# Rearranging the last sixty microseconds of a streaming decode kernel: transfer order, deferred work, a direct last P.V, and closer weight columns

## The chip, the cores and the metric

The kernel runs on one core of a Trainium2 chip. The metric is the device time of one execution in microseconds (us). The profile's span, which runs from the first to the last recorded event, is about 1.8 us shorter than the time of the same execution.

## The reference, cut to what matters

One token goes through a transformer layer. The parts that matter are the sizes.

```
x: 1 x 512                      32 query heads, 8 key/value heads, head size 128
k_cache, v_cache: 8 x 65536 x 128, bf16   (134 MB each)
mod = silu(c) @ w_mod           -> six vectors of 512
h   = layernorm(x) * (1+ca) + sa
q   = h @ wq                    (512 x 4096)
o   = softmax(q k^T / sqrt(128)) v        for each of the 32 heads
x   = x + ga * (o @ wo)         (4096 x 512)
h2  = layernorm(x) * (1+cb) + sb
x   = x + gb * ((silu(h2 @ w_gate) * (h2 @ w_up)) @ w_down)     (512 x 1792, 1792 x 512)
```

Every weight and every cached key and value is read once: 285.48 MB. The output is one row of 512 numbers.

## The kernel before

The caches are cut into 32 chunks of 16384 keys, four to each key/value head. One chunk of K is 4 MB and so is one of V. All large transfers are issued from one queue (SyncE) in a fixed order, a list called `stream`. A store in SBUF of 24 units holds six chunks; `pump` issues the next transfer of the list as soon as enough neighbouring units have been given back by `done`.

```python
UNIT = 4096
UNITS = 24
V_END = (0, 64, 96, 112, 128)               # the last V comes in four pieces
PV_RUNS = ((10, 0, 16), (14, 16, 32))
# ...
    for i in range(NCH + 2):                # NCH = 32 chunks
        if i >= 2:
            kv("v", A_v_cache, i - 2, V_END if i - 2 == NCH - 1 else (0, NB))
        if i < NCH:
            kv("k", A_k_cache, i)
        if NCH + 1 - len(wo_at) <= i <= NCH:
            g0 = wo_at[i - (NCH + 1 - len(wo_at))]
            w(("o", g0), wo3, g0, g0 + WO_G)
    w(("g",), B_w_gate.rearrange("(p k) n -> p k n", p=P), 0, KC)
    w(("u",), B_w_up.rearrange("(p k) n -> p k n", p=P), 0, KC)
    w(("d",), B_w_down.rearrange("(p k) n -> p k n", p=P), 0, FC, (0, FC0, FC))
```

So the end of the stream is ..., V29, K31, (output weights), V30, (output weights), V31, w_gate, w_up, w_down.

For every chunk TensorE transposes K, computes scores, and multiplies the softmax weights P with V. That last product ("P.V") is done as 32 wide matmuls. Each takes four blocks of keys at once and so leaves a 128 x 512 result, of which only matching blocks are wanted. VectorE copies it, and four small matmuls in fp32 (`pv_fold`; the trace counts them as eight) pick out and add the wanted parts.

```python
    def pv_one(cc, q4):
        nc.tensor.matmul(out=pvw[32 * jt:32 * jt + QB * rep, :],
                         lhsT=pt_of[cc][:, b0:b0 + QB, :].rearrange("p b h -> p (b h)"),   # 16 columns
                         rhs=held[("v", cc)][:, b0:b0 + QB, :].rearrange("p j d -> p (j d)"),  # 512
                         # ...
        if q4 == NQ - 1:
            done(("v", cc))
            nc.vector.tensor_copy(out=pvw_sb[:], in_=pvw[:])
```

After the last chunk this has to be followed, one thing after the other, by the copy, the fold, the weights of the four chunks (`head_out`), a turn of the result (`head_turn`), the output projection of the last head, the layernorm, w_gate and w_up, the activation, w_down, and the output transfer.

The feed-forward weights are used as the stationary side of 128 x 128 matmuls with one moving column (`gemv`). Of each row of w_gate and w_up, one matmul takes the columns `strided(held[key][:, kc, :], FC)[:, :, nb]`. With FC = 14 these are every 14th column.

## Time and profile before

| | before |
|---|---|
| median of the first six runs | 693.92 us (692.95 to 696.38) |
| span of the profiled run | 693.8 us |
| bytes streamed | 285.48 MB |
| last V piece landed | 665.2 us |
| last w_down piece landed | 678.1 us |
| h2 (the input of w_gate and w_up) ready | 680.8 us |

These are the lines of the page of the kernel before on which this rests. The row "DMA" is the busy share of the 16 DMA engines in tenths, in 40 slices of the span; the queue lines give packets, MB, and the share of the 16 engines' time.

```profile
span 693.8 us, 18060 instructions
...
DMA  9999999999999999999999999999999999999960
...
q1 hardware_dynamic: 11648, 285.48, 96.2%
q8 instruction: 63, 1.03, 0.6%
```

The stream fills all slices but the last two: the kernel is bound by its input for 660 us and by something else for the rest. The queue q8 carries instructions, not data.

The next view of the kernel before cuts the end into stretches. Its columns are the stretch, its length, the busy time of PE (with its number of instructions), PEld, DVE, ACT and POOL, the granted TensorE clock, the DMA share, and GB/s.

```profile
400.00:500.00 100.00, 89.83 (x1207) 78.12 (x1204) 41.42 (x89) 31.17 (x82) 0.00 (x0) 0.74 1.00 429
660.00:665.00 5.00, 2.30 (x31) 1.86 (x28) 2.61 (x10) 0.93 (x5) 0.00 (x0) 0.74 0.99 406
665.00:670.00 5.00, 4.28 (x118) 4.26 (x122) 0.71 (x4) 2.17 (x7) 0.00 (x0) 0.50 0.63 264
670.00:675.00 5.00, 4.20 (x40) 1.59 (x38) 0.69 (x1) 0.00 (x0) 0.00 (x0) 0.59 0.51 210
675.00:680.00 5.00, 1.94 (x23) 1.67 (x24) 1.98 (x11) 0.21 (x1) 0.48 (x1) 0.64 0.15 58
680.00:685.00 5.00, 4.15 (x70) 4.15 (x70) 0.62 (x3) 0.00 (x0) 0.08 (x1) 0.50 0.00 0
```

In the body the DMA engines are at 1.00 and move 429 GB/s. From 665 us on the share is near one half, although there is still data to move: some of the 16 engines have finished and others have not. Each of the 78 transfers of queue q1 is split over 16 engines (the trace has 1248 closing packets of 4 bytes, 16 for each), and the trace has the time at which each engine finished its share. For the last piece of w_down these 16 times are, sorted:

```
665.0 665.1 665.1 665.2 665.6 665.9 669.4 671.9 675.8 675.9 677.3 677.4 677.4 677.5 677.6 678.1
```

Six engines end at 665 us and eight at about 677. What waits for a transfer here waits for the slowest engine. So the end of the stream (called E) is 678.1 us and not 665.

The last view of the kernel before is its timeline of the tail. The columns are start, busy time (both in us), engine, line, operation, what is written from what, the shape, the number of instructions, and in brackets how long the engine had been idle and what ended that.

```profile
652.78 1.58 PE L371 MATMUL pvw<-store,pt 128*16 128x512 bf16 x16 [3.72 <-DMA store<-in_A_v_cache_dram]
...
666.17 3.86 PE L472 MATMUL attn_ps<-oF,store 128*128 128x1 bf16 x112
669.96 3.59 PE L371 MATMUL pvw<-store,pt 128*16 128x512 bf16 x32
673.61 0.69 DVE L379 COPY pvw_sb<-pvw 128x512 f32<-128x512 f32 x1 [6.35 <-PE pvw L371]
674.35 1.15 PE L389 MATMUL oc<-sel,pvw_sb 128*128 128x4 f32 x8 [0.80 <-DVE pvw_sb L379]
...
676.94 0.67 PE L472 MATMUL attn_ps<-oF,store 128*128 128x1 bf16 x16 [0.25 <-DVE oF L429]
...
680.64 0.16 DVE L518 TENSOR_TENSOR h2T<-m,modT 128x4 bf16<-128x4 f32 x1
680.85 6.83 PE L205 MATMUL gu_ps<-h2T,store 128*128 128x1 bf16 x112 [1.73 <-DVE h2T L518]
688.77 2.03 PE L539 MATMUL f_ps<-guT,store 128*128 128x1 bf16 x56
691.58 0.36 SPq L548 DMA_DIRECT2D out_dram<-o_bf  x1
```

TensorE last waits long for data at 652.78 us, when V30 lands. After that it works through scores, projection and P.V in the order of the program. From the last scores (661.6) to 665.7 us it mostly waits: in three waits of 0.78, 0.62 and 2.01 us for VectorE and ScalarE, which make the softmax of the last chunk. The projection of seven heads doesn't need that softmax, but it stands behind it in the program. When the last V piece is there (665.2), TensorE isn't free for it until 669.96. Note also the two rates: 112 matmuls of the output projection (columns 4 apart) take 3.86 us, which is 34 ns each, and 112 of w_gate and w_up (columns 14 apart) take 6.83 us, 61 ns each.

### The profile page before, as it was taken

What the parts mean: (1) busy time and instruction counts of PE and PEld (TensorE: products, weight loads), DVE (VectorE), ACT (ScalarE), POOL (GpSimd) and SP (SyncE); (2) the same over time, 40 slices, a digit from 0 to 9 for tenths busy, and PEclk for the clock granted to TensorE, in tenths of its full rate; (3) what the DMA queues carried; (4) which work ended last, traced back from release to release, by engine and by line L of the source; (5) the groups of instructions that cost most, each with busy time, mean ns of one, the idle gap of its engine ahead of it and who ended that gap; (6) DMA issues with size and microseconds to landing.
All of it is one profiled execution on the core that took longest, in us unless ns stands there. A gap on an engine that the chain in (4) does not pass through costs nothing.

```text
span 693.8 us, 18060 instructions
## 1 busy us (share of the span) xinstructions
PE 582.6 (84%) x8084; PEld 505.6 (73%) x8084; DVE 264.0 (38%) x604; ACT 200.1 (29%) x527; POOL 3.6 (1%) x17
## 2 busy tenths in 40 slices
PE   1599897988989898988889799888988998887776
PEld 1588786777878787877777688777876787776655
DVE  2154344433434335343444345333443433432331
ACT  0043133332322333333223233332323332321310
POOL 1000000000000000000000000000000000000000
PEclk9988778775867768687768868776877776877765
DMA  9999999999999999999999999999999999999960
GB/s 387 423 423 436 431 427 428 429 429 432 426 430 431 428 435 422 427 433 433 426 424 437 427 427 427 430 431 428 431 425 434 429 428 425 421 435 425 413 289 5
DMA packets 11729, 286.63 MB, mean 413 GB/s; under 512 B 1282, under 2 KB 1284, under 8 KB 2692
## 3 DMA queue, kind: packets, MB, share of 16 engines
q1 hardware_dynamic: 11648, 285.48, 96.2%
q8 instruction: 63, 1.03, 0.6%
q14 instruction: 14, 0.11, 0.0%
q10 hardware_dynamic: 4, 0.00, 0.0%
HBM read 285.48 MB, written 0.00 MB: 411 GB/s over the span
## 4 chain that ended last, share of the span: by engine, by line
issue 97%; PE 2%; DMA 1%; DVE 0%; POOLq 0%; POOL 0%; ACTq 0%; ACT 0%
PE gu_ps L205 1%; DMA store<-in_A_x_dram 1%; PE f_ps L539 0%; PE ln_tot L215 0%; POOLq L574 0%; PE ln_var L224 0%; POOL ln_rstd L228 0%; ACTq L158 0%; DVE xn L513 0%; PE xc_ps L188 0%; PE o_ps L545 0%; PE o_ps L533 0%; DVE xd L218 0%; ACT sg L526 0%; DVE gu_bf L524 0%
## 5 line engine op out<-in xcount | busy, mean ns | idle before, releaser
L308 PE MATMUL ktp<-ident_f,store 128*128 128x128 f32 x2048 | 393.1, 325 | 54.5 <-DMA store<-in_A_k_cache_dram 54.4
L308 PEld LDWEIGHTS ktp<-ident_f,store 128*128 128x128 f32 x2048 | 255.1, 160 | 88.4 <-issue 83.1
L314 DVE COPY kts<-ktp 128x512 int32<-128x512 int32 x256 | 177.1, 692 | 305.4 <-PE ktp L308 304.5
L312 ACT COPY kts<-ktp 128x512 f32<-128x512 f32 x256 | 151.2, 591 | 450.9 <-PE ktp L308 448.6
L329 PEld LDWEIGHTS <-kts 128*128 128x128 bf16 x4096 | 196.1, 102 | 16.6 <-ACT kts L312 1.4
L329 PE MATMUL st<-qpair,kts 128*128 128x8 bf16 x4096 | 185.1, 169 | 1.2 <-ACT kts L312 1.2
L371 PE MATMUL pvw<-store,pt 128*16 128x512 bf16 x1024 | 76.4, 427 | 13.9 <-DMA store<-in_A_v_cache_dram 13.8
L361 ACT ACTIVATE pt<-st,negb 128x128 bf16<-128x128 f32 x128 | 51.2, 556 | 5.5 <-DVE negb L354 5.4
L371 PEld LDWEIGHTS <-pt 128*16 128x16 bf16 x1024 | 22.4, 94 | 33.0 <-issue 17.0
L379 DVE COPY pvw_sb<-pvw 128x512 f32<-128x512 f32 x32 | 22.1, 692 | 44.7 <-PE pvw L371 44.7
L389 PE MATMUL oc<-sel,pvw_sb 128*128 128x4 f32 x256 | 36.4, 265 | 1.0 <-DVE pvw_sb L379 0.8
L389 PEld LDWEIGHTS oc<-sel,pvw_sb 128*128 128x128 f32 x256 | 33.6, 206 | 4.5 <-DVE pvw_sb L379 1.7
L361 ACT ACTIVATION_READ_ACCUMULATOR pt<-st,negb 128x1 f32 x128 | 36.3, 283 | 0.0
L205 PEld LDWEIGHTS <-store 128*128 128x128 bf16 x336 | 13.9, 127 | 13.7 <-DMA store<-in_A_wq_dram 8.5
L336 DVE TENSOR_REDUCE mx<-st 128x4 f32<-128x512 f32 x32 | 21.8, 681 | 0.2 <-PE st L329 0.2
L341 PE MATMUL mt<-ident_f,mx 128*4 128x128 f32 x32 | 10.5, 329 | 9.8 <-DVE mx L336 8.2
L351 PE MATMUL mb<-dg,ones_f 4*128 4x4 f32 x64 | 14.1, 289 | 0.6 <-DVE dg L345 0.6
L343 DVE TENSOR_REDUCE m<-mt 4x1 f32<-4x128 f32 x32 | 8.9, 279 | 13.5 <-PE mt L341 13.5
L351 PEld LDWEIGHTS mb<-dg,ones_f 4*128 4x128 f32 x64 | 11.3, 220 | 1.7 <-DVE dg L345 0.8
L391 DVE COPY oT<-oc 128x4 f32<-128x4 f32 x32 | 5.2, 162 | 18.1 <-PE oc L389 18.1
L341 PEld LDWEIGHTS mt<-ident_f,mx 128*4 128x4 f32 x32 | 2.6, 82 | 12.6 <-DVE mx L336 12.6
L205 PE MATMUL q_ps<-m_h,store 128*128 128x1 bf16 x128 | 3.6, 165 | 8.5 <-DMA store<-in_A_wq_dram 8.5
(98 smaller groups left out, 87.2 us busy)
## 6 DMA issues: line engine op xcount, KB each, us to landing
store<-in_A_k_cache_dram SPq DMA_DIRECT2D x32, 4096.0 KB, 43.4
store<-in_A_v_cache_dram SPq DMA_DIRECT2D x31, 4096.0 KB, 52.3
store<-in_A_wq_dram SPq DMA_DIRECT2D x1, 4096.0 KB, 19.5
store<-in_A_wo_dram SPq DMA_DIRECT2D x4, 1024.0 KB, 46.0
store<-in_w_mod_dram SPq DMA_DIRECT2D x1, 3072.0 KB, 10.2
store<-in_A_v_cache_dram SPq DMA_DIRECT2D x1, 2048.0 KB, 45.6
store<-in_B_w_gate_dram SPq DMA_DIRECT2D x1, 1792.0 KB, 29.6
store<-in_B_w_up_dram SPq DMA_DIRECT2D x1, 1792.0 KB, 31.4
```

The costliest lines, as they stand in the source:

```text
L205: nc.tensor.matmul(out=out_ps[:, nb:nb + 1], lhsT=lhs(kc, nb), rhs=actT[:, kc:kc + 1], start=(kc == 0), stop=(kc == n_kc - 1))
L308: nc.tensor.transpose(out=ktp[:, e4, :], in_=kt32[:, j0:j0 + 2, :].rearrange("p a i -> p (a i)"), identity=ident_f[:])
L312: nc.scalar.copy(out=kts[:].bitcast(F32), in_=ktp[:])
L314: nc.vector.tensor_copy(out=kts[:].bitcast(I32), in_=ktp[:].bitcast(I32))
L329: nc.tensor.matmul(out=st[:, b0:b0 + 2, :].rearrange("p b h -> p (b h)"), lhsT=ktsv[:, e4, :, e], rhs=qpair[:, g, e, :, :].rearrange("p j ...
L336: nc.vector.tensor_reduce(out=mx[:], in_=st_of[cc][:].rearrange("p b h -> p h b"), axis=AX.X, op=ALU.max)
L341: nc.tensor.transpose(out=mt[:], in_=mx[:], identity=ident_f[:])
L351: nc.tensor.matmul(out=mb[:], lhsT=ones_f[0:rep, :], rhs=dg[:], start=True, stop=True)
L361: nc.scalar.activation(out=pt_of[cc][:, :, h], in_=st_of[cc][:, :, h], func=ACT.Exp, bias=negb[:, h:h + 1], scale=scale, accum_out=Lp[:, c ...
L371: nc.tensor.matmul(out=pvw[32 * jt:32 * jt + QB * rep, :], lhsT=pt_of[cc][:, b0:b0 + QB, :].rearrange("p b h -> p (b h)"), rhs=held[("v", ...
L379: nc.vector.tensor_copy(out=pvw_sb[:], in_=pvw[:])
L389: nc.tensor.matmul(out=oc_ps[:], lhsT=pvw_sb[:, bl * Dh:(bl + 1) * Dh], rhs=sel[:, bl, :], start=(bl == 0), stop=(bl == QB - 1))
```

## The change

The intent is to have less work left when the last data arrives. There are four parts.

1. The store's units are halved (48 of 2048), so that smaller transfers fit more tightly. It still holds six chunks.
2. The end of the transfer order changes. The last K goes ahead of V29. P.V of chunks 29 and 30 is deferred: it runs after the last scores instead of among them.
3. The last chunk's P.V is done directly: 128 matmuls with a block of V as the stationary side and 4 columns of P moving. The result has the form that the output projection needs, so the copy, the fold and the turn are gone. The last head's output weights come in a layout to match, in 1 KB packets.
4. The matmuls of w_gate and w_up take columns 4 apart instead of 14 (2 apart in the last 256 columns). w_down's rows are arranged to match, and come in three pieces.

```diff
-UNIT = 4096
-UNITS = 24
+UNIT = 2048
+UNITS = 48
-V_END = (0, 64, 96, 112, 128)
+V_END = (0, 64, 112, 128)
 # ... transfer order
+    order[order.index(("v", NCH - 3)):] = [("k", NCH - 1), ("v", NCH - 3), ("ol",),
+                                           *(o for o in order[order.index(("k", NCH - 1)):] if o[0] == "o"),
+                                           ("v", NCH - 2), ("v", NCH - 1)]
 # ... columns of w_gate and w_up, 4 apart
+    fblocks = [(f0, min(4, (F - f0) // P)) for f0 in range(0, F, 4 * P)]
+    def fcols(w2):
+        return [w2[:, f0:f0 + e * P].rearrange("p (m e) -> p m e", e=e)[:, :, i] for f0, e in fblocks for i in range(e)]
 # ... when P.V runs
+        if cc == NCH - 1:
+            continue
+        if cc == NCH - 3:
+            runs = [END, END + 1]
+        if cc == NCH - 2:
+            runs = [END + 7, END + 8]
 # ... the projection of seven heads between them
+    at(END + 3, attn_begin)
 # ... the last chunk
+    for b in range(NB):
+        nc.tensor.matmul(out=ol_ps[:], lhsT=v_l[:, b, :], rhs=pt_l[:, b, :], start=(b == 0), stop=(b == NB - 1))
+    nc.vector.tensor_tensor(out=ol[:], in0=ol_ps[:], in1=wgt[:, NCPH - 1, :], op=ALU.mult)
+    nc.vector.tensor_tensor(out=ol_bf[:], in0=ol[:], in1=rest[:], op=ALU.add)
+    for nb in range(KC):
+        for h in range(rep):
+            nc.tensor.matmul(out=attn_ps[:, nb:nb + 1], lhsT=strided(wl[:, h, :], KC)[:, :, nb],
+                             rhs=ol_bf[:, h:h + 1], start=False, stop=(h == rep - 1), skip_group_check=True)
 # ... rest of the change cut: the loading of w_down and of the last head's output weights
```

`END` is the step of the last scores.

More of the change, by code (lines that the diff above doesn't have):

```diff
@@ L90, in room @@
         fits = [u for u in range(0, UNITS - n + 1, n) if all(free[u:u + n])]
-        return min(fits, key=lambda u: (sum(free[u // 4 * 4:u // 4 * 4 + 4]), u)) if fits else None
+        return min(fits, key=lambda u: (sum(free[u // 8 * 8:u // 8 * 8 + 8]), u)) if fits else None
     def pump():
@@ L133, in load @@
             return v
-        stream.append((key, max((k1 - k0) * n, 4 * UNIT if key == ("mod",) else 0), load))
+        stream.append((key, max((k1 - k0) * n, 8 * UNIT if key == ("mod",) else 0), load))
     w(("mod",), w_mod.rearrange("(p k) n -> p k n", p=P), 0, KC)
     w(("q",), A_wq.rearrange("(p k) n -> p k n", p=P), 0, KC)
+    GROWS = rep * Dh
     wo3 = A_wo.rearrange("(g p j) n -> p g (j n)", p=P, j=rep)
-    wo_at = list(range(0, Hkv, WO_G))
-    for i in range(NCH + 2):
+    wo_last = A_wo[(Hkv - 1) * GROWS:, :].rearrange("(h d) n -> d h n", d=P)
@@ L141 @@
+    wo_at = {max(0, NCH - 4 + i): (g0, min(g0 + WO_G, Hkv - 1)) for i, g0 in enumerate(range(0, Hkv - 1, WO_G))}
+    order = []
+    for i in range(NCH):
         if i >= 2:
-            kv("v", A_v_cache, i - 2, V_END if i - 2 == NCH - 1 else (0, NB))
-        if i < NCH:
-            kv("k", A_k_cache, i)
-        if NCH + 1 - len(wo_at) <= i <= NCH:
-            g0 = wo_at[i - (NCH + 1 - len(wo_at))]
-            w(("o", g0), wo3, g0, g0 + WO_G)
+            order.append(("v", i - 2))
+        order.append(("k", i))
+        if i in wo_at:
+            order.append(("o", *wo_at[i]))
@@ new lines @@
+    order[order.index(("v", NCH - 3)):] = [("k", NCH - 1), ("v", NCH - 3), ("ol",),
+                                           *(o for o in order[order.index(("k", NCH - 1)):] if o[0] == "o"),
+                                           ("v", NCH - 2), ("v", NCH - 1)]
+    for o in order:
+        if o[0] == "k":
+            kv("k", A_k_cache, o[1])
+        elif o[0] == "v":
+            kv("v", A_v_cache, o[1], V_END if o[1] == NCH - 1 else (0, NB))
+        elif o[0] == "o":
+            w(("o", o[1]), wo3, o[1], o[2])
+        else:
+            w(("ol",), wo_last, 0, rep)
@@ L148, with d_load @@
     w(("g",), B_w_gate.rearrange("(p k) n -> p k n", p=P), 0, KC)
     w(("u",), B_w_up.rearrange("(p k) n -> p k n", p=P), 0, KC)
-    FC0 = FC - 4
-    w(("d",), B_w_down.rearrange("(p k) n -> p k n", p=P), 0, FC, (0, FC0, FC))
-    at0 = 3 * UNIT
+    fblocks = [(f0, min(4, (F - f0) // P)) for f0 in range(0, F, 4 * P)]
+    def fcols(w2):
+        return [w2[:, f0:f0 + e * P].rearrange("p (m e) -> p m e", e=e)[:, :, i] for f0, e in fblocks for i in range(e)]
+    def d_load(t):
+        v = t[:, 0:FC * D].rearrange("p (j n) -> p j n", n=D)
+        full = [f0 for f0, e in fblocks if e == 4]
+        nf = len(full)
+        for b0, b1 in ((0, nf - 1), (nf - 1, nf)):
+            nc.sync.dma_start(out=v[:, 4 * b0:4 * b1, :].rearrange("p (b e) n -> p b (e n)", e=4),
+                              in_=B_w_down[b0 * 4 * P:b1 * 4 * P, :].rearrange("(b p e) n -> p b (e n)", p=P, e=4))
+        if FC > 4 * nf:
+            nc.sync.dma_start(out=v[:, 4 * nf:FC, :].rearrange("p e n -> p (e n)"),
+                              in_=B_w_down[nf * 4 * P:F, :].rearrange("(p e) n -> p (e n)", p=P))
+        return v
@@ L154 @@
+    FC0 = FC // 4 * 4
+    stream.append((("d",), FC * D, d_load))
+    at0 = 6 * UNIT
     c_row = store[0:1, at0:at0 + D]
@@ L442 @@
     NBANKS = NCH * BPC
-    TAIL_AT = NBANKS + S_LAG + 6
-    def late(step):
-        return step if step < NBANKS else step + TAIL_AT - NBANKS
+    END = NBANKS + S_LAG - 1
     for cc in range(NCH):
@@ L454 @@
             at(e + 3 + h // 2, lambda cc=cc, h=h: sm_exp(cc, carry[("nb", cc)], h))
-        for i, a, b in PV_RUNS:
-            at(late((cc + 1) * BPC + i), lambda cc=cc, a=a, b=b: pv_run(cc, a, b))
-        p1 = late((cc + 1) * BPC + PV_RUNS[-1][0] + 1)
+        g = cc // NCPH
+        if cc % NCPH == NCPH - 1:
+            at(e + 6, keep(("wgt", g), lambda g=g: head_weights(g)))
+        if cc == NCH - 1:
+            continue
+        runs = [(cc + 1) * BPC + i for i, _, _ in PV_RUNS]
+        if cc == NCH - 3:
+            runs = [END, END + 1]
+        if cc == NCH - 2:
+            runs = [END + 7, END + 8]
+        for step, (_, a, b) in zip(runs, PV_RUNS):
+            at(step, lambda cc=cc, a=a, b=b: pv_run(cc, a, b))
+        p1 = runs[-1] + 1
         at(p1, lambda cc=cc: pv_fold(cc))
         if cc % NCPH == NCPH - 1:
-            g = cc // NCPH
-            at(e + 6, keep(("wgt", g), lambda g=g: head_weights(g)))
             at(p1 + 1, keep(("om", g), lambda wgt, g=g: head_out(g, wgt), ("wgt", g)))
@@ L473, in wo_part @@
                                      rhs=oF[:, g, j:j + 1], start=(g == 0 and j == 0 and nb == 0),
-                                     stop=(g == Hkv - 1 and j == rep - 1), skip_group_check=True)
+                                     stop=False, skip_group_check=True)
     def attn_begin():
@@ L479, in attn_begin @@
         wo_part(0, Hkv - 1)
-    side.setdefault(TAIL_AT, []).insert(0, attn_begin)
+    at(END + 3, attn_begin)
     last = max(side)
@@ L489 @@
             fn()
-    wo_part(Hkv - 1, Hkv)
-    for g0 in range(0, Hkv, WO_G):
+    gl = Hkv - 1
+    wgt = carry.pop(("wgt", gl))
+    oT = heads.pop(gl)[2]
+    rest = once.tile([P, rep], F32, name="rest", tag="rest")
+    if NCPH > 1:
+        ow = once.tile([P, NCPH - 1, rep], F32, name="ow_l", tag="ow_l")
+        nc.vector.tensor_tensor(out=ow[:], in0=oT[:, 0:NCPH - 1, :], in1=wgt[:, 0:NCPH - 1, :], op=ALU.mult)
+        nc.vector.tensor_reduce(out=rest[:], in_=ow[:].rearrange("p c h -> p h c"), axis=AX.X, op=ALU.add)
+    else:
+        nc.vector.memset(rest[:], 0.0)
+    v_l, pt_l = held[("v", NCH - 1)], pt_of.pop(NCH - 1)
+    ol_ps = pmisc.tile([P, rep], F32, name="ol_ps", tag="misc")
+    for b in range(NB):
+        nc.tensor.matmul(out=ol_ps[:], lhsT=v_l[:, b, :], rhs=pt_l[:, b, :], start=(b == 0), stop=(b == NB - 1))
+    done(("v", NCH - 1))
+    ol = once.tile([P, rep], F32, name="ol", tag="ol")
+    nc.vector.tensor_tensor(out=ol[:], in0=ol_ps[:], in1=wgt[:, NCPH - 1, :], op=ALU.mult)
+    ol_bf = once.tile([P, rep], BF16, name="ol_bf", tag="ol_bf")
+    nc.vector.tensor_tensor(out=ol_bf[:], in0=ol[:], in1=rest[:], op=ALU.add)
+    wl = held[("ol",)]
+    for nb in range(KC):
+        for h in range(rep):
+            nc.tensor.matmul(out=attn_ps[:, nb:nb + 1], lhsT=strided(wl[:, h, :], KC)[:, :, nb],
+                             rhs=ol_bf[:, h:h + 1], start=False, stop=(h == rep - 1), skip_group_check=True)
+    for g0 in range(0, Hkv - 1, WO_G):
         done(("o", g0))
+    done(("ol",))
     warm = once.tile([P, 1], F32, name="warm", tag="warm")
@@ L520 @@
     for i, key in enumerate((("g",), ("u",))):
-        gemv(gu_ps[:, i, :], lambda kc, nb: strided(held[key][:, kc, :], FC)[:, :, nb], h2T, KC, FC)
+        cols = [fcols(held[key][:, kc, :]) for kc in range(KC)]
+        gemv(gu_ps[:, i, :], lambda kc, nb: cols[kc][nb], h2T, KC, FC)
         done(key)
@@ L535 @@
     wd_sb = held[("d",)]
-    for f0, f1 in ((0, FC0), (FC0, FC)):
+    for f0, f1 in ((0, FC0 - 4), (FC0 - 4, FC0), (FC0, FC)):
         for nb in range(KC):
```

## The prediction

> **What bounds the kernel.** The inbound DMA stream. The queue table shows 285.48 MB on one queue, 96% of 16 engines' span; the stretches from 40 to 640 us all read 429 GB/s at a DMA share of 1.00. [...]
>
> The engines do not end together. Each transfer's 16 completion events show eight engines about 12 us behind the fastest at the end. The last weights (w_down) land between 665.0 and 678.1 us; from 665 on the DMA share is near 0.5. The instruction queue (63 packets of 16 KB, 1.07 us each) may explain most of the lag. The laggards set the end of the stream, E = 678.1 us.
>
> From E to the end of the span (693.8 us) is 15.7 us, and that is exposed compute. The timeline of the tail: attention output weights 666.2-670.0, last P.V 670.0-673.6 (its last V piece had landed at 665.2), copy, fold, head output and last output projection to 677.6, layernorm to 680.8, gate and up 6.8 us, activation and setup 1.1, down 2.0, final combination 0.75, output DMA 2.2.
>
> **What the change does.** Bytes and engines' work are the same, so E should stay, plus about 0.3 us: 1 KB packets take 45 ns and 4 KB ones 161 ns, against 1215 for 32 KB (packet records), and the last output weights and w_down now come in smaller packets. The finer units keep six 4 MB blocks; the body does not change.
>
> The last K is moved ahead of two V blocks, landing about 5 us earlier (near 633), and two P.V passes move behind the last scores. Then projection of seven heads and P.V of chunk 30 run while V31 is landing (660-665). V31 goes straight through 128 four-column matmuls piece by piece; I estimate 35 ns each, from the output projection's 112 in 3.9 us. The fold, head turn and transposition vanish: after the last V piece about 0.6 (last 16 blocks) + 0.6 + 0.7 (output projection) + 3.2 (layernorm) us, so h2 is ready near 671, possibly 672, not 680.8. Gate lands near 669.4, up near 673.7. Gate and up drop from 61 ns a matmul (columns 14 elements apart) to about 35 (4 apart, as the down matmuls: 56 in 2.0 us): 6.8 becomes 4 us. Up ends near 675.8, activation near 676.9, down 2.0 us more, almost together with E.
>
> **Sum.** Compute after E shrinks from 15.7 to about 3.5-4 us: end near 681.9 us of span, 12 us less. E is a floor. Predicted 682.0 us (-1.7%), just short of 2%.
>
> **Signs.** E at 677-679; landing of w_down last, and the down matmuls waiting for it; gate/up near 35 ns; P.V of chunk 31 waiting for V pieces, not for TensorE; body at 429 GB/s; no idle DMA before 664.
>
> **What would make it wrong.** Direct P.V at 60 ns at the half clock (stretches after 664 read PEclk 0.5) would delay h2 to about 674 and add 2 us. Deferred P.V passes might hold V blocks so long that w_down is issued late. Fewer instruction fetches on the laggards near the end could bring E forward by 1-2 us and carry it past 2%.
>
> Chances: faster by over 2% 0.18, within 2% 0.81, slower 0.01. Range 679.6 to 685.0.

## The result, and the profile after

The kernel after took 683.37 us (median of 8 runs, 682.97 to 683.71) against 694.24 us of the kernel before (16 runs, 692.95 to 696.38). The ratio is 0.9844, with a 95% interval of 0.9833 to 0.9855: the change is 1.6% faster, which is within 2%. Ratios in this document are the mean time of one kernel's runs over that of the other's runs of the same rounds, so they are not quite the ratio of the medians that are quoted.

The page of the kernel after, the same lines:

```profile
span 681.6 us, 18237 instructions
...
DMA  8999999999999999999999999999999999999994
...
q1 hardware_dynamic: 12176, 285.48, 98.0%
q8 instruction: 64, 1.05, 0.6%
```

The bytes are the same, the idle slices at the end are nearly gone, and there is one more packet of instructions. The same stretches of the kernel after:

```profile
400.00:500.00 100.00, 90.41 (x1203) 79.33 (x1202) 41.16 (x90) 31.46 (x82) 0.00 (x0) 0.80 1.00 428
660.00:665.00 5.00, 4.09 (x125) 4.00 (x126) 0.77 (x4) 0.00 (x0) 0.00 (x0) 0.78 0.99 407
665.00:670.00 5.00, 1.89 (x42) 1.77 (x39) 1.96 (x11) 0.21 (x1) 0.55 (x1) 0.50 0.61 254
670.00:675.00 5.00, 3.36 (x102) 3.27 (x101) 0.00 (x0) 0.00 (x0) 0.00 (x0) 0.50 0.51 206
675.00:680.00 5.00, 2.90 (x74) 2.62 (x71) 0.78 (x5) 0.21 (x1) 0.00 (x0) 0.50 0.19 73
```

The DMA columns of the first four rows agree with those before to 4%: the stream was not made faster, in its body or in its end. What changed is what TensorE does beside it. The clock of this profiled run was 0.823 on average and that of the profiled run before 0.763. But the runs of the kernel before that had clocks of 0.81 to 0.84 took 693.01 to 695.58 us, all over 9 us more than any run of the kernel after, so the clock is not what the change did.

The timeline of the tail of the kernel after:

```profile
647.70 1.90 PE L400 MATMUL pvw<-store,pt 128*16 128x512 bf16 x32
...
651.70 3.89 PE L506 MATMUL attn_ps<-oF,store 128*128 128x1 bf16 x112
655.97 3.55 PE L400 MATMUL pvw<-store,pt 128*16 128x512 bf16 x32
...
661.24 1.76 PE L538 MATMUL ol_ps<-pt,store 128*128 128x4 bf16 x64
663.59 1.87 PE L538 MATMUL ol_ps<-pt,store 128*128 128x4 bf16 x64 [0.59 <-DMA store<-in_A_v_cache_dram]
665.91 0.68 PE L547 MATMUL attn_ps<-ol_bf,store 128*128 128x1 bf16 x16 [0.45 <-DVE ol_bf L543]
669.61 0.17 DVE L576 TENSOR_TENSOR h2T<-m,modT 128x4 bf16<-128x4 f32 x1
669.83 1.95 PE L234 MATMUL gu_ps<-h2T,store 128*128 128x1 bf16 x56 [1.74 <-DVE h2T L576]
673.42 1.98 PE L234 MATMUL gu_ps<-h2T,store 128*128 128x1 bf16 x56 [1.64 <-DMA store<-in_B_w_up_dram]
...
676.49 2.03 PE L598 MATMUL f_ps<-guT,store 128*128 128x1 bf16 x56
679.30 0.36 SPq L607 DMA_DIRECT2D out_dram<-o_bf  x1
```

The projection of seven heads, which ran from 666 to 670 us, now runs from 652 to 656, before the last V is there. It and P.V of chunk 29 fill the time in which the last chunk's softmax is made (until about 654 us). P.V of the last chunk waits for V and not V for TensorE. And between the two halves of line 234 there is a wait for w_up's landing: TensorE has caught up with the stream. Side by side, read from the two traces:

| us from the start of the span | before | after |
|---|---|---|
| scores of the last chunk done | 661.6 | 647.8 |
| last V piece landed | 665.2 | 664.8 |
| P.V of the last chunk done | 673.6 | 665.5 |
| last output projection done | 677.6 | 666.6 |
| h2 ready | 680.8 | 669.8 |
| w_up landed | 673.7 | 673.4 |
| w_gate and w_up used | 687.7 | 675.4 |
| last w_down piece landed (E) | 678.1 | 677.8 |
| w_down used | 690.8 | 678.5 |
| end of the span | 693.8 | 681.6 |

### The profile page after: what moved, and what is told of

It reads as the page before. It is cut to its first block, busy times and chain, and to the rows that moved or that the text cites. A ratio compares the mean times of both kernels' runs of the same rounds, so it can differ in the third digit from the quotient of the medians.

```text
span 681.6 us, 18237 instructions
## 1 busy us (share of the span) xinstructions
PE 578.7 (85%) x8171; PEld 508.7 (75%) x8171; DVE 262.3 (38%) x602; ACT 201.8 (30%) x527; POOL 3.6 (1%) x17
## 3 DMA queue, kind: packets, MB, share of 16 engines
q1 hardware_dynamic: 12176, 285.48, 98.0%
q8 instruction: 64, 1.05, 0.6%
## 4 chain that ended last, share of the span: by engine, by line
DMA 66%; PE 29%; DVE 2%; issue 1%; ACT 1%; another core or an unknown queue 0%; SPq 0%; DVEq 0%; ACTq 0%
DMA store<-in_A_k_cache_dram 55%; PE ktp L337 18%; DMA store<-in_A_v_cache_dram 7%; PE st L358 5%; DMA store<-in_B_w_up_dram 5%; PE pvw L400 4%; DVE kts L343 1%; DVE mx L365 1%; PE mb L380 1%; PE mt L370 1%; PE oc L418 0%; PE gu_ps L234 0%; PE f_ps L598 0%; ACT pt L390 0%
## 5 line engine op out<-in xcount | busy, mean ns | idle before, releaser
L337 PE MATMUL ktp<-ident_f,store 128*128 128x128 f32 x2048 | 398.0, 327 | 57.6 <-DMA store<-in_A_k_cache_dram 57.6
L337 PEld LDWEIGHTS ktp<-ident_f,store 128*128 128x128 f32 x2048 | 266.2, 165 | 85.2 <-issue 78.3
L400 PE MATMUL pvw<-store,pt 128*16 128x512 bf16 x992 | 67.2, 395 | 4.5 <-DMA store<-in_A_v_cache_dram 4.4
L400 PEld LDWEIGHTS <-pt 128*16 128x16 bf16 x992 | 20.5, 90 | 22.1 <-issue 7.3
L418 PE MATMUL oc<-sel,pvw_sb 128*128 128x4 f32 x248 | 32.7, 255 | 2.4 <-DVE pvw_sb L408 1.4
L418 PEld LDWEIGHTS oc<-sel,pvw_sb 128*128 128x128 f32 x248 | 30.0, 191 | 6.1 <-DVE pvw_sb L408 2.5
L234 PEld LDWEIGHTS <-store 128*128 128x128 bf16 x336 | 10.7, 112 | 15.4 <-DMA store<-in_A_wq_dram 8.6
L380 PE MATMUL mb<-dg,ones_f 4*128 4x4 f32 x64 | 15.6, 312 | 0.1
L380 PEld LDWEIGHTS mb<-dg,ones_f 4*128 4x128 f32 x64 | 12.8, 249 | 1.4
```

Of the source, the lines that this page charges most:

```text
L234: nc.tensor.matmul(out=out_ps[:, nb:nb + 1], lhsT=lhs(kc, nb), rhs=actT[:, kc:kc + 1], start=(kc == 0), stop=(kc == n_kc - 1))
L337: nc.tensor.transpose(out=ktp[:, e4, :], in_=kt32[:, j0:j0 + 2, :].rearrange("p a i -> p (a i)"), identity=ident_f[:])
L380: nc.tensor.matmul(out=mb[:], lhsT=ones_f[0:rep, :], rhs=dg[:], start=True, stop=True)
L400: nc.tensor.matmul(out=pvw[32 * jt:32 * jt + QB * rep, :], lhsT=pt_of[cc][:, b0:b0 + QB, :].rearrange("p b h -> p (b h)"), rhs=held[("v", ...
L418: nc.tensor.matmul(out=oc_ps[:], lhsT=pvw_sb[:, bl * Dh:(bl + 1) * Dh], rhs=sel[:, bl, :], start=(bl == 0), stop=(bl == QB - 1))
```

## The experiments

The theory to be tested is that of the prediction. The stream's end stays where it is, and the whole gain is compute that no longer comes after it, in three shares: the order with the deferral, the direct P.V, the columns. The first rival is that one share does it all, or that the shares do not depend on each other. The second question is why the stream's end stays at 678 us when six of its engines are done at 665. The theory there is the instruction fetch; the rival is that these engines are slow for the data itself.

### One share taken away

The kernel after with the columns 14 apart again:

```diff
-        cols = [fcols(held[key][:, kc, :]) for kc in range(KC)]
-        gemv(gu_ps[:, i, :], lambda kc, nb: cols[kc][nb], h2T, KC, FC)
+        gemv(gu_ps[:, i, :], lambda kc, nb: strided(held[key][:, kc, :], FC)[:, :, nb], h2T, KC, FC)
```

> The changed kernel with the columns of gate and up read 14 elements apart again (w_down's rows to match, still in three pieces). Theory (the stream's end near 678 us is a floor, and only what comes after the landing of w_up is exposed): gate's 56 matmuls grow from 2.0 to 3.4 us but hide before w_up lands at 673.4; only up's 1.4 us shows: 684.8 us. Rival (the parts of the change simply add up): the full 2.9 us of both: 686.3 us. Rival (the gain came from a faster stream): no change, 683.4 us.

Measured: 684.95 us, ratio to the kernel before 0.9875 (0.9859 to 0.9892), against 0.9844. Its timeline has one group for w_gate and w_up:

```profile
669.62 7.12 PE L234 MATMUL gu_ps<-h2T,store 128*128 128x1 bf16 x112 [1.74 <-DVE h2T L576]
```

h2 was ready at the same time, and the 112 matmuls took 7.12 us without a wait for w_up in between. With close columns they take 3.93 us, but with 1.64 us of waiting. So 1.6 us of the 3.2 us that close columns save reach the end; the rest becomes a wait for w_up.

The kernel after with the old P.V, copy, fold and turn for the last chunk, and its old output weights:

```diff
-        if cc == NCH - 1:
-            continue
+        if cc == NCH - 1:
+            runs = [END + 10, END + 11]
 # ... the 128 direct matmuls and the separate last projection taken out
+    wo_part(Hkv - 1, Hkv)
```

> The changed kernel with the last chunk's P.V by the old way (32 wide matmuls, copy, fold, head output, turn, old layout of the last output weights); new order and new gate/up kept. Theory: h2 comes near 672.7 us of span and not 669.8, of which 1.6 us hide behind the landing of w_up; 1.3 us show: 684.7 us. Rival (parts add up): the whole 2.9 us: 686.3 us.

Measured: 685.33 us, ratio 0.9888 (0.9871 to 0.9904), so about 2.0 us are lost.

```profile
666.63 1.87 PE L418 MATMUL oc<-sel,pvw_sb 128*128 128x4 f32 x8 [0.79 <-DVE pvw_sb L408]
...
673.65 0.16 DVE L552 TENSOR_TENSOR h2T<-m,modT 128x4 bf16<-128x4 f32 x1
```

h2 came at 673.8 us, 1 us later than expected. Most of that is the fold, which took 1.87 us here and not the 1.15 us that it had taken in the kernel before. The granted clock was 0.50 in this stretch and 0.85 at the fold of the kernel before. Again only half of the 4.0 us by which h2 is late reach the end.

The kernel after with the old order and without deferral:

```diff
-    order[order.index(("v", NCH - 3)):] = [("k", NCH - 1), ("v", NCH - 3), ("ol",),
-                                           *(o for o in order[order.index(("k", NCH - 1)):] if o[0] == "o"),
-                                           ("v", NCH - 2), ("v", NCH - 1)]
+    order.append(("v", NCH - 2))
+    order += [("ol",), ("v", NCH - 1)]
-        if cc == NCH - 3:
-            runs = [END, END + 1]
-        if cc == NCH - 2:
-            runs = [END + 7, END + 8]
```

> The changed kernel with the old order of transfers (last K after V of chunk 29, no P.V deferred); direct P.V, new gate/up and split w_down kept. Theory: scores of the last chunk end near 661.6 us as before, direct P.V near 671.6, h2 near 676, and nothing waits for w_up any more: 4.5 us later, 687.9 us; w_down lands at the same 678 us. Rival (order of transfers cannot matter where bytes are the bound; the gain is shorter compute): within 1 us of 683.4.

Measured: 687.97 us, ratio 0.9918 (0.9903 to 0.9933), 4.6 us lost.

```profile
663.76 3.89 PE L501 MATMUL attn_ps<-oF,store 128*128 128x1 bf16 x112
...
676.24 0.16 DVE L571 TENSOR_TENSOR h2T<-m,modT 128x4 bf16<-128x4 f32 x1
```

The projection of seven heads is back at 664 us, where the last V is landing, and everything behind it is late.

### One share alone

The kernel before with close columns and nothing else (the edit is the part of the change's diff that concerns `fcols` and w_down):

```diff
-        gemv(gu_ps[:, i, :], lambda kc, nb: strided(held[key][:, kc, :], FC)[:, :, nb], h2T, KC, FC)
+        cols = [fcols(held[key][:, kc, :]) for kc in range(KC)]
+        gemv(gu_ps[:, i, :], lambda kc, nb: cols[kc][nb], h2T, KC, FC)
```

> The kernel before with only the new gate/up columns (4 apart) and the w_down rows and pieces that go with them. Theory: all weights have landed by 678.1 us when gate starts at 680.9, so the whole saving of both, 112 matmuls from 61 to 35 ns, 2.9 us, shows here: 693.6 to 690.7 us. In the changed kernel the same edit is worth 1.6 us (measured when it was taken back). Rival (one and the same worth wherever it stands): 1.6 us, 692.0 us.

Measured: 691.02 us against 693.68, ratio 0.9956 (0.9934 to 0.9978), a gain of 2.7 us.

```profile
678.27 3.76 PE L221 MATMUL gu_ps<-h2T,store 128*128 128x1 bf16 x112 [1.73 <-DVE h2T L534]
```

3.76 us instead of 6.83, all of it on the critical path, since w_up had landed at 673.1, before h2 was ready. The same edit is worth 2.7 us here and 1.6 us in the kernel after. The traces give three prices for a matmul with one moving column: 61 ns with its weight columns 14 apart, about 35 ns with them 4 apart, and 28 ns with them next to each other (128 matmuls with wq in 3.57 us, at a granted clock of 1.00). What makes the distance cost time is not shown. The clock doesn't explain these steps: the 61 and the 35 ns of w_gate and w_up were both measured at a granted clock of 0.50, and the two halves of the direct P.V, whose columns are next to each other, took 28 ns a matmul at 0.94 and 29 at 0.50.

The kernel before's P.V and columns with the new order and deferral alone. It was made from the kernel after, so the halved units and w_down in three pieces stayed; the lines are those in which its order differs from that of the kernel before:

```diff
+    order[order.index(("v", NCH - 3)):] = [("k", NCH - 1), ("v", NCH - 3),
+                                           *(o for o in order[order.index(("k", NCH - 1)):] if o[0] == "o"),
+                                           ("v", NCH - 2), ("v", NCH - 1)]
+        if cc == NCH - 3:
+            runs = [END, END + 1]
+        if cc == NCH - 2:
+            runs = [END + 7, END + 8]
+        if cc == NCH - 1:
+            runs = [END + 10, END + 11]
```

> The new order and the deferred P.V alone: old P.V of the last chunk, old gate/up columns. Theory: h2 near 672.7, then gate and up at 61 ns a matmul, 6.8 us, to 679.5; the end 4.1 us after the changed kernel's: 687.5 us, so order alone brings about 6.5 of the 11 us. Rival (shorter compute brought most): less than half of the gain is left, above 689 us.

Measured: 688.27 us, ratio 0.9924 (0.9909 to 0.9938). The order with the deferral gains about 5.3 us, about half of what the whole change gains; 687.5 us had been expected.

Together: the shares gain 2.7 us (columns alone) and 5.3 us (order alone), and taking them away from the whole costs 1.6, 2.0 and 4.6 us. The three costs add up to about 8 us and not to 10.9. That is what a floor does. In the kernel after w_up's landing stands in the way, so the last step towards it is worth less than it would be elsewhere.

Two things were not run: the direct P.V alone, and the halved units alone. No run separates the units from the rest. The landings give them little to do with the stream (last V at 665.2 and 664.8 us, E at 678.1 and 677.8), but whether the new order would gain as much without them is not shown.

### Early K and deferral apart

The order and the deferral are two things. First the early K without the deferral:

```diff
-        if cc == NCH - 3:
-            runs = [END, END + 1]
-        if cc == NCH - 2:
-            runs = [END + 7, END + 8]
```

> The changed kernel with the last K still ahead of two V blocks, but the P.V of chunks 29 and 30 back at their old places among the scores. Theory: TensorE runs in order, so the last scores wait behind P.V of chunk 30 for a V that lands near 655 us; scores end near 661, as when order and deferral were both undone (687.97 us): 687.5 to 688.5 us, the early K alone is worth nothing. Rival (the early K brings the gain): near 683.4 to 684.5 us.

Measured: 693.65 us, ratio 0.9997 (0.9983 to 1.001). The expectation missed by 5 us, and the time is worse than with neither (687.97).

```profile
642.06 1.88 PE L400 MATMUL pvw<-store,pt 128*16 128x512 bf16 x16 [13.01 <-DMA store<-in_A_v_cache_dram]
...
681.50 0.16 DVE L572 TENSOR_TENSOR h2T<-m,modT 128x4 bf16<-128x4 f32 x1
```

TensorE took its instructions in the order of the program here. K31 came early (632.3 us in the kernel after, which has the same order of transfers), but before the last scores the program has P.V of chunk 29, and V29 now comes after K31. TensorE stood for 13.01 us before a block that had been put behind.

Then the deferral without the early K:

```diff
-    order[order.index(("v", NCH - 3)):] = [("k", NCH - 1), ("v", NCH - 3), ("ol",),
-                                           *(o for o in order[order.index(("k", NCH - 1)):] if o[0] == "o"),
-                                           ("v", NCH - 2), ("v", NCH - 1)]
+    order.append(("v", NCH - 2))
+    order += [("ol",), ("v", NCH - 1)]
```

> The changed kernel with the two P.V passes deferred behind the last scores, but the last K back behind V of chunk 29. Theory: the last K lands near 642.5 and its scores take 11.5 us, to 654; P.V 29, seven heads' projection, P.V 30 and direct P.V then follow one another on TensorE, h2 near 675.6: 687.5 us, so deferral alone is worth 0.5 of the 4.6 us that both bring together. Rival (deferral brings the gain): near 683.4 to 684.5 us.

Measured: 691.60 us, ratio 0.9967 (0.9950 to 0.9985), again a miss, by 4 us.

```profile
642.39 1.08 PE L336 MATMUL ktp<-ident_f,store 128*128 128x128 f32 x4 [7.78 <-DMA store<-in_A_k_cache_dram]
...
678.68 0.16 DVE L575 TENSOR_TENSOR h2T<-m,modT 128x4 bf16<-128x4 f32 x1
```

Here TensorE is idle for 7.78 us before K31, with V29 in the store and P.V of chunk 29 put off until later. The work that would have filled the wait comes after it.

| medians, us | K31 in its old place | K31 early |
|---|---|---|
| P.V of chunks 29 and 30 among the scores | 687.97 | 693.65 |
| P.V of chunks 29 and 30 after them | 691.60 | 683.37 |

Each half alone loses 3.6 or 5.7 us, and both together gain 4.6. The order of arrival and the order of work have to be changed together.

### Why eight DMA engines lag

The instruction queue's 64 packets hold 1.05 MB. The trace has 8171 matmuls, each of two instructions (weights, then columns). 1.05 MB over these 16342 instructions is 64 bytes for each, and the first run below agrees: it has 2048 matmuls fewer and 16 packets of 16384 bytes fewer, which is 64 bytes for an instruction too. So, by this estimate, nearly all of the fetched code is TensorE's (8171 matmuls make 1.046 MB). The trace does not say which DMA engine carried a packet; 64 packets on eight engines would be eight to each. Whether these packets hold up the data is what the next two runs ask. The first leaves out one of the two score matmuls of each pair. Its output is wrong, which doesn't matter for the time.

```diff
-            for e in range(2):
+            for e in range(1):
-                                 start=(e == 0), stop=(e == 1))
+                                 start=(e == 0), stop=(e == 0))
```

> Wrong result on purpose: the changed kernel with every second score matmul left out, 2048 fewer pairs of weight load and matmul. Theory (eight DMA engines lag because they also fetch TensorE's instructions): 2048 x 2 x 64 bytes are 16 packets of 16 KB fewer, 64 to 48; at 1.07 us each over 8 engines the laggards end 2.1 us earlier, 677.8 to 675.7, the fastest engines stay near 665, and the time falls to 681.3 us. Rival (those engines are slower by themselves): the last landing stays at 677.8, 683.4 us.

The second goes the other way. It writes each wide P.V matmul as two of 256 columns, with the same result.

```diff
+        for h0 in (0, QB // 2):
+            nc.tensor.matmul(out=pvw[32 * jt:32 * jt + QB * rep, h0 * Dh:(h0 + QB // 2) * Dh],
+                             # ... the same lhsT
+                             rhs=held[("v", cc)][:, b0 + h0:b0 + h0 + QB // 2, :].rearrange("p j d -> p (j d)"),
```

> The changed kernel with every P.V matmul of 512 columns made as two of 256: 992 more pairs of weight load and matmul, same result. Fetch theory: 7 to 8 packets of 16 KB more (64 to 72), the last landing 1.0 us later, 678.8, 684.4 us; the fastest engines stay near 665. Rival (no link between instructions and lag): 677.8 and 683.4 us. If TensorE became the bound instead, the DMA share of the body would fall below 1.

Measured: 680.45 us, ratio 0.9804 (0.9786 to 0.9821), with half the scores, 2.9 us less than the kernel after. 685.22 us, ratio 0.9872 (0.9851 to 0.9893), with split P.V, 1.8 us more. The queue lines of the two pages, first with half the scores:

```profile
q8 instruction: 48, 0.79, 0.5%
```

and with split P.V:

```profile
q8 instruction: 71, 1.16, 0.7%
```

The 16 completion times of the last w_down piece, sorted:

```
half the scores, 48 packets:
664.8 665.1 665.2 665.3 665.4 665.6 668.9 671.7 672.7 674.2 674.3 674.3 674.4 674.5 674.7 674.8
kernel after, 64 packets:
664.9 665.1 665.3 665.3 665.6 665.7 669.3 671.7 675.9 677.2 677.3 677.3 677.4 677.5 677.6 677.8
split P.V, 71 packets:
664.8 664.9 665.0 665.1 665.3 665.4 669.2 671.7 677.3 678.7 678.8 678.9 679.0 679.1 679.2 679.6
```

The first eight of the sorted times agree from list to list within 0.4 us, so the stream as a whole was not paced differently by TensorE's lighter or heavier work. The last eight move with the number of packets. 16 packets fewer, which is two for each of these engines, moved E by 3.0 us, so by this estimate a packet costs its engine 1.5 us, although its own record lasts 1.07 us. The traces also have a check in which the number of TensorE's instructions stays the same. Only packets that are fetched before the late engines end can delay them. Up to 675.5 us, 63 of the 64 packets of the kernel after have started, and one engine ends a packet early (675.9). In the kernel before it is 62 of 63, and two engines are early (675.8 and 675.9). The run with the early K alone has as many matmuls as the kernel after, but only 61 packets by then, and three engines are early (675.6, 675.8 and 675.9). This is what 63, 62 and 61 packets dealt out in turn to eight engines would give, and the seven other runs whose stream ends near 678 us agree. Eight packets at 1.5 us are 12 us, and 677.3 less 12 is 665.3, where the six quick engines end. So the rival falls: the instruction fetch accounts for the lag of these eight engines. (That the packets are spread evenly over just these eight is worked out from the lists, not read.) The two engines at 669 and 671.7 us did not move with the packets; what holds those back stays open.

The last run of this group is meant to give the eight laggards less data. It loads three V chunks by parts of their partitions (rows 0 to 112, then two times eight).

```diff
+            rows = (0, 112, 120, 128) if (cache is A_v_cache and i in SHIFT) else (0, P)
             for j0, j1 in zip(cuts, cuts[1:]):
-                nc.sync.dma_start(out=v[:, j0:j1, :], in_=src[:, j0:j1, :])
+                for p0, p1 in zip(rows, rows[1:]):
+                    nc.sync.dma_start(out=v[p0:p1, j0:j1, :], in_=src[p0:p1, j0:j1, :])
```

The edit reckons with 16 engines for 112 rows and 8 engines for 8 rows. The trace agrees: each engine that takes part in a transfer ends it with a packet of 4 bytes (the kernel after has 1264, 16 for each of its 79 transfers), and this run has 48 of these more than the kernel after (12224 packets of queue q1 and not 12176), eight for each of the six transfers of 8 rows.

> The changed kernel with three V blocks (chunks 20, 22, 24) loaded as 112 partitions on 16 engines and 2 x 8 partitions, each on 8 engines[...]. If the eight that lag are those that are relieved, the last landing comes 2.5 to 3.6 us earlier, near 674.5 to 675.3, and the time falls to 680 to 681 us. If they are those that are loaded, it comes 3.6 us later, 681.4, and the time rises to 687 us. Rival (the lag is no matter of load on an engine): no change.

The 2.5 to 3.6 us are the estimate: up to three packets of 32 KB, at 1.215 us by the packet records, more or less on an engine.

Measured: 769.56 us, ratio 1.1088 (1.106 to 1.1116). Neither expectation came near.

```profile
360.00:400.00 40.00, 34.70 (x473) 30.37 (x472) 15.21 (x31) 12.21 (x32) 0.00 (x0) 0.84 1.01 430
...
560.00:600.00 40.00, 20.65 (x238) 17.72 (x237) 8.94 (x23) 6.49 (x18) 0.00 (x0) 0.66 1.00 201
...
640.00:680.00 40.00, 35.10 (x461) 30.76 (x459) 15.28 (x34) 12.43 (x33) 0.00 (x0) 0.74 1.01 430
```

From about 425 to 610 us the engines stay busy (share near 1.00) but move far less, 201 GB/s in the stretch shown, and then recover. As the share stayed high, the engines were not short of transfers: each packet took longer, up to 4.8 us for 32 KB (at most 1.9 us otherwise). Why the packets took longer is not shown. Whether the laggards were relieved can't be read from this run, so the remedy was not tested.

### A shorter tail

The kernel after waits for w_up's landing, then works 8.2 us until the end. The next kernel brings w_up in two halves, so that half of its matmuls can run before the rest lands, and writes the output from 128 partitions, without the two small matmuls and the copy at the end.

```diff
+    w(("u",), B_w_up.rearrange("(p k) n -> p k n", p=P), 0, KC, (0, KC // 2, KC))
 # ... gate and up: k-halves outside, columns inside; the first small matmul taken out
-    nc.tensor.matmul(out=o_ps[:], lhsT=of[:], rhs=t3[:].rearrange("p s k -> p (s k)"), start=False, stop=True)
-    nc.vector.tensor_copy(out=o_bf[:], in_=o_ps[:])
+    nc.vector.tensor_tensor(out=t3[:], in0=f_ps[:], in1=gbT, op=ALU.mult)
+    nc.vector.tensor_tensor(out=o_bf[:], in0=t3[:], in1=x1T[:], op=ALU.add)
+    nc.sync.dma_start(out=out.rearrange("a b (p k) -> (a b p) k", k=KC), in_=o_bf[:])
```

> The changed kernel with w_up in two halves by contraction rows, so that half its matmuls run before its last landing, and with the output written straight from 128 partitions (no fold to 32 partitions before it). Theory: two chains are balanced after the change, from w_up's landing (673.4, 8.2 us to the end) and from w_down's (677.8, 3.5 us); this shortens the first by 1 to 1.5 us and the second by 0.3, so only 0.5 to 0.7 us show against the changed kernel of the same call. Rival (w_up's landing alone limits): 1 to 1.5 us.

The kernel after was run again beside it, on the same chip:

> The changed kernel again, on the same chip as the other three, to compare them with: 683.4 us.

Measured: 681.26 us (680.98 to 682.70), ratio to the kernel before 0.9821 (0.9806 to 0.9837), against 683.49 us and 0.9848 (0.9835 to 0.9862) of the kernel after. It is the quickest correct kernel, but not for the reason for which it was written.

```profile
672.43 2.27 PE L597 MATMUL f_ps<-guT,store 128*128 128x1 bf16 x56 [1.40 <-DMA store<-in_B_w_down_dram]
675.12 0.35 SPq L605 DMA_DIRECT2D out_dram<-o_bf  x1
```

In its profiled run the whole stream is quicker. The quickest engine ends at 662.7 us instead of 664.9, and E is 674.2 instead of 677.9. The number of instruction packets is the same (64), but each took 934 ns on average instead of 1063, and a data packet of 32 KB 1217 ns instead of 1221. The lead grows all along: 0.7 us after 100 MB, 1.7 after 200, 3.0 after 280. An edit of the last 10 us does not explain that, and why it is so stays open. What the edit itself did is mixed. The wait has moved from w_up to w_down, as intended. But the output transfer, 128 pieces of 8 bytes, took 3.0 us to land where 32 pieces of 32 bytes had taken 1.4 us. From E to the end of the span there are now 5.0 us, not 3.8. The intervals of the two kernels meet, and the ratio of the two, 0.9821 over 0.9848, is 0.997.

## Why the prediction was right or wrong

The prediction gave 682.0 us with a range of 679.6 to 685.0, and most of the chance to "within 2%". The median was 683.37 us. The mechanism held, with one wait misnamed.

- **"E should stay."** It did: 678.1 before, 677.8 after, and 677.5 to 678.1 in the runs that took a share of the change away, made one alone, or ran the kernel after again, in whatever order they loaded or worked. The one exception is the shorter tail (674.2), whose whole stream was quicker for a reason that stays open. "The body does not change" held too: 429 and 428 GB/s.
- **"The projection of seven heads and P.V of chunk 30 run while V31 is landing."** They ran at 652 to 659.5 us, just before V31's last pieces. P.V of chunk 31 then waited 0.59 us for V, as the signs had asked for. K31 landed at 632.3 us, near the 633 that had been said, though that is 7.5 us earlier than before (639.8) and not 5. h2 was ready at 669.8, where 671 had been said.
- **"Gate and up drop from 61 ns to about 35."** 56 matmuls took 1.95 and 1.98 us, 35 ns each. With only that part, the kernel before gained 2.7 us.
- **"The instruction queue may explain most of the lag."** The two runs with fewer and more instructions showed it for the eight late engines, and more strongly than the prediction had it: a packet costs 1.5 us and not the 1.07 us of its record.

Some steps of the sum were off, though their errors stayed small.

- **"The down matmuls waiting for" w_down** did not happen. The 56 ran without a gap from 676.49 us. What TensorE waited for was w_up, 1.64 us, until 673.42; the end of the span is that landing plus 8.2 us of work. By an estimate from the same trace, a kernel bound by w_down would end at E plus the last matmuls and the output, 677.8 + 3.5 = 681.3 us, only 0.3 us earlier than it did. The prediction's own timetable has the path through w_up (landed near 673.7, used by 675.8, activation near 676.9, then 2.0 us of w_down); its sum and its signs named E instead. The two limits lie so close together that the time came out right with the wrong one named. The run with the shorter tail did wait for w_down.
- **"I estimate 35 ns each" for the direct P.V** was a little high: 64 took 1.76 us, 28 ns each. The estimate came from matmuls whose columns lie 4 apart; a block of V has its columns next to each other. For h2 this hardly mattered, since only the last blocks are left when V has landed. That h2 came at 669.8 and not at 671 is mostly rounding: the prediction's own terms after the last V piece (665.2) add up to 670.3, and that piece landed 0.4 us earlier than before.
- **"12 us less"** mixes two things. It was read from the trace of one run, which at 695.54 us was 1.6 us above the median of its six, and subtracted from the median. The spans did differ by 12.2 us (693.8 to 681.6), but the medians by 10.9 (694.24 to 683.37). This is nearly all of the 1.4 us by which the prediction was low.
- **"From E to the end is 15.7 us, and that is exposed compute."** The length is right, but E did not start that stretch. In the kernel before, the work that ends last, followed back by its waits in the timeline, goes back to the landing of V30 at 652.7 us, and no step of it waits for w_down. E became a limit only when the work ahead of it was gone. The runs that took a share away agree: without the direct P.V h2 came 4.0 us later and the end 2.0 us, without the order 6.6 and 4.6 us.

The prediction also treated the early K and the deferred P.V as one thing, which they are. But it said nothing of what either would do alone, and the expectations for those two runs were 4 and 5 us too low. Both reckoned with TensorE going through its program in order; they misjudged where it would stand. For the early K alone the expectation had the scores wait for V30. But V29 had been put behind K31 too, and the wait for it (13.01 us) came first, so the last scores ended at 666.8 us and not near 661. For the deferral alone the scores of K31 took 14.3 us (642.4 to 656.7) and not 11.5, which is most of the 3.1 us by which h2 came late. By an estimate, about half of that is the clock: after the wait it was 0.50 for 3 us, and the first three groups of K31's 16 took 1.14 us each against 0.68 for the later ones at 1.00, which makes 1.4 us.

## What to carry to other kernels

At the end of a kernel that is bound by its input, list what each landing releases, and arrange transfers and work together so that little is left behind the last landing; moving only one of the two can cost more than it gains (here it lost 3.6 or 5.7 us). When such a kernel's DMA engines do not end together, look at who else uses the late ones: here it was the fetch of TensorE's instructions, so that fewer instructions moved the end, with the same bytes of data (16 packets fewer, 3.0 us). Take a predicted saving off the run that it was read from, and only then compare with medians.
